# Pooled attention with a mixture of adapters: query transposes from 16 rows of 128 tokens, and score matmuls that read the queries in permuted order

## The chip, the cores and the metric

The kernel runs on one core of a Trainium2 chip. The metric is device time in microseconds (us) of one execution, at the median of several. The profiler's span is some 2 us shorter than that time. "Granted clock" is the TensorE clock that the throttle allowed, as a share of full speed, averaged over a stretch. In the traces its records are 1.00 or 0.50 only, so a value in between says for how much of the stretch the clock was halved.

## The reference, cut to what matters

```python
# q: (4, 12288, 128)   kv: (4, 384, 32, 128)   all float32
kv_pool = kv.reshape(B, H//4, 4, W//4, 4, C).mean(axis=(2, 4))   # 768 keys per batch entry
k = v = kv_pool.reshape(B, -1, C) @ w_sr
a = softmax(q @ k.T / sqrt(C));  x = a @ v                        # 49152 tokens of 128
# then per token: gate logits, the best 2 of 8 adapters of rank 16, x + weighted deltas
```

Each token is computed from its own query. The output for a token must land in that token's row, so a kernel may take tokens in any order as long as loads and stores agree.

The comparison with the reference hardly sees the order of the tokens. Worked out from the reference's own outputs, the tokens of one batch entry differ from their mean by 2.6e-6 (root mean square), where the outputs themselves have a spread of 5.0e-4. For the changed kernel and for the version with runs of 16, the token order was therefore checked by following the indices through transpose, read and store; it is right in both.

## The kernel before: the parts that the change and the argument touch

Queries are cast to bf16 in DRAM in groups of 2048 tokens (`GT`), transposed by one DMA instruction per group into `qT` (128 channels on partitions, tokens along the free axis), and used in chunks of 512 tokens (`T`, four to a group, 96 chunks in all). Groups 0 and 1 are loaded as float32 and transposed by TensorE instead.

```python
def load_qT(g):
    t = qpool.tile([P, GT], BF16, tag="qT", name="qT")
    keep(nc.sync.dma_start(t.rearrange("c (j p) -> c j p", p=P),
                           q_bf[g].rearrange("(p j) c -> p (j c)", p=P), transpose=True))

def load_q(g, lo, hi):                       # groups 0 and 1 only
    src = q[0, g * GT:(g + 1) * GT].rearrange("(p j) c -> p j c", p=P)
    keep(nc.sync.dma_start(q_f[g][:, lo:hi], src[:, lo:hi]))

def scores(k, r):                            # 3 calls per chunk, 2 matmuls each
    rhs = qT[k // GC][:, (k % GC) * T:(k % GC + 1) * T]        # 512 adjacent bf16
    ps = ps_s.tile([P, 2, T], FP32, tag="sg", name="sg")
    for i in range(2):
        mm(ps[:, i], kfT[b][:, 2 * r + i], rhs, start=True, stop=True)
    keep(nc.scalar.activation(em[k][:, 2 * r:2 * r + 2], ps, AF.Exp, bias=0.0, scale=scale))

def attend(k, s):                            # em is the weight, vx the moving operand: acc
    for j in range(J):
        mm(o, em[k][:, j, s * P:(s + 1) * P], vx[b][:, j], start=(j == 0), stop=(j == J - 1))

# ... normalize (xn), gates on GpSimd, transposes (tt_ps), down (h_ps), gate (hg), up (d_ps) ...

def finish(k):                               # partition p stores 4 adjacent tokens: 2 KB runs
    keep(nc.sync.dma_start(
        out[k // GC * GT:(k // GC + 1) * GT].rearrange("(p j) c -> p j c", p=P)
        [:, k % GC * S:(k % GC + 1) * S], osb))
```

The softmax here doesn't subtract the row's maximum and nothing guards it: scores larger than these inputs give would overflow.

## Time and profile before

| | before |
|---|---|
| time, median of 2 | 426.77 us |
| TensorE busy, share of the span | 92% |
| granted clock, mean | 0.979 |
| one chunk in the steady state | 3.68 us |
| one pair of score matmuls | 0.43 us |

The busy times of the page of before, whole span:

```profile
PE 389.1 (92%) x4589; PEld 308.8 (73%) x4589; DVE 327.3 (77%) x967; ACT 292.8 (69%) x336; POOL 162.5 (38%) x263
```

Busy times by stretch, before. The columns are the stretch and its length, then busy time (and instructions) of each engine, the granted clock, the DMA engines' busy share and GB/s:

```profile
core 0: us, PE busy (x) PEld busy (x) DVE busy (x) ACT busy (x) POOL busy (x), PEclk, DMA share, GB/s
...
100.00:145.00 45.00, 45.00 (x563) 36.46 (x561) 39.23 (x114) 34.07 (x39) 12.14 (x25) 1.00 0.70 174
...
200.00:245.00 45.00, 45.00 (x563) 36.48 (x560) 39.02 (x113) 34.91 (x40) 12.15 (x23) 1.00 0.71 184
```

The average of 92% hides that TensorE is busy in all of these stretches (45.00 of 45.00 us), at full clock (1.00). How long each instruction holds it there the busy time does not say, so the next view is the chain of waits, the chain that ended last. Columns: start, length, instructions. This is one period of before:

```profile
329.47 0.43 PE sg L68 x2
329.90 0.22 PE h_ps L68 x4
330.12 1.12 PE acc L68 x18
331.24 0.43 PE sg L68 x2
331.67 0.45 PE tt_ps L68 x8
332.12 0.43 PE sg L68 x2
332.55 0.22 PE d_ps L68 x4
332.77 0.37 PE acc L68 x6
333.15 0.43 PE sg L68 x2
```

From 329.47 to 333.15 is 3.68 us, and nothing but matmuls is on it. A pair of score matmuls (`sg`) takes 0.43 us, so 215 ns for 512 columns, or 0.42 ns a column. The list of groups gives another number for the same instruction (columns: busy time, mean ns of one, then the idle time before and who ended it):

```profile
L68 PE MATMUL sg<-qT,kfT 128*128 128x512 bf16 x576 | 170.9, 378 | 2.7 <-ACT em L246 2.2
L246 ACT ACTIVATE em<-sg 128x1024 f16<-128x1024 f32 x288 | 280.5, 1023 | 97.3 <-PE sg L68 96.4
```

The 378 ns are the time from start to end of one matmul; in the chain the next one starts 215 ns after it. For the cost in a stream, use the distances in the chain.

The DMA side of before (packets, then issues with KB each and median us from issue to landing):

```profile
DMA packets 71172, 76.43 MB, mean 181 GB/s; under 512 B 49904, under 2 KB 50160, under 8 KB 70640
...
qT<-qbf SPq DMA_TRANSPOSE x22, 8.1
```

A transpose lands 8.1 us after its issue and is used about a group (four chunks, 14.7 us) later. No compute engine's list of waits shows one for it.

### The profile page before, as it was taken

The page shows a single profiled execution, that of the slowest core. Times are in us where ns is not written, and L with a number is a line of the kernel's source. Part 1 is how long each engine was busy: PE and PEld are TensorE (multiplying, and loading weights), DVE is VectorE, ACT ScalarE, POOL GpSimd, SP SyncE. Part 2 cuts the span into 40 slices and gives each one's busy share as a digit, 9 for nine tenths or more (in the row PEclk, how much of TensorE's full clock was granted, in tenths as well). Part 3 has the DMA queues.
Part 4 walks back from the last instruction along what each step waited for, and adds up shares of the span by engine and source line. Part 5 has one row for each costly group of instructions (what it writes and reads, how often), then busy time and mean ns, then how long its engine had stood idle before and what let it go on. Part 6 is the DMA issues. An engine that isn't in the chain of part 4 may idle for free.

```text
span 423.3 us, 11396 instructions
## 1 busy us (share of the span) xinstructions
PE 389.1 (92%) x4589; PEld 308.8 (73%) x4589; DVE 327.3 (77%) x967; ACT 292.8 (69%) x336; POOL 162.5 (38%) x263
## 2 busy tenths in 40 slices
PE   4898999999999999999999999999999999999853
PEld 3566777787877878787888778777888877788642
DVE  2644678788988878779888878779888888888853
ACT  3478567686777777676788777676777866678522
POOL 0010357965320557964330467963231312222000
PEclk9999999999999999999999999999999999999965
DMA  8989557776556998765647999998575628342112
GB/s 302 397 214 284 110 182 199 276 161 140 128 123 134 335 252 258 286 159 114 158 126 150 318 248 164 355 135 182 130 170 129 150 76 175 108 119 75 52 63 88
DMA packets 71172, 76.43 MB, mean 181 GB/s; under 512 B 49904, under 2 KB 50160, under 8 KB 70640
## 3 DMA queue, kind: packets, MB, share of 16 engines
q1 hardware_dynamic: 70128, 64.11, 52.7%
q0 software_dynamic: 704, 11.54, 14.5%
q8 instruction: 36, 0.59, 0.6%
q14 instruction: 16, 0.13, 0.1%
q10 hardware_dynamic: 288, 0.07, 0.1%
HBM read 50.53 MB, written 36.70 MB: 206 GB/s over the span
## 4 chain that ended last, share of the span: by engine, by line
PE 72%; DVE 10%; POOL 8%; ACT 3%; DMA 2%; issue 2%; SPq 1%; ACTq 0%; DVEq 0%
PE acc L68 28%; PE sg L68 23%; PE tt_ps L68 9%; PE d_ps L68 5%; PE h_ps L68 4%; POOL kvr L171 4%; DVE hg L350 3%; ACT em L246 2%; DVE osb L363 2%; DVE xn L263 2%; POOL over L293 1%; PE v_ps L68 1%; SPq L98 1%; PE kpT_ps L68 1%; DMA kvr<-in_kv_dram 1%
## 5 line engine op out<-in xcount | busy, mean ns | idle before, releaser
L246 ACT ACTIVATE em<-sg 128x1024 f16<-128x1024 f32 x288 | 280.5, 1023 | 97.3 <-PE sg L68 96.4
L68 PE MATMUL acc<-vx,em 128*128 128x137 f16 x2304 | 174.1, 224 | 2.0 <-DVE xn L263 1.9
L68 PE MATMUL sg<-qT,kfT 128*128 128x512 bf16 x576 | 170.9, 378 | 2.7 <-ACT em L246 2.2
L68 PEld LDWEIGHTS <-em 128*128 128x128 f16 x2304 | 149.8, 98 | 4.9 <-DVE xn L263 2.2
L68 PEld LDWEIGHTS <-tts 128*128 128x128 bf16 x768 | 59.1, 99 | 53.0 <-ACT tts L334 5.6
L350 DVE TENSOR_TENSOR hg<-h_ps,gw 128x512 bf16<-128x512 f32 x96 | 66.1, 688 | 29.9 <-POOL gw L315 16.1
L293 POOL TENSOR_TENSOR over<-xn,srt 128x128 f32<-128x128 f32 (+1 forms) x54 | 19.8, 384 | 175.7 <-DVE srt L281 175.7
L263 DVE TENSOR_TENSOR xn<-acc,rinv 128x544 f32<-128x544 f32 x96 | 69.5, 724 | 3.3
L171 POOL TENSOR_TENSOR kvr<-kvr 128x512 f32<-128x512 f32 x54 | 67.4, 1268 | 2.1 <-DMA kvr<-in_kv_dram 1.9
L363 DVE TENSOR_TENSOR osb<-d_ps,xn 128x512 f32<-128x512 f32 x96 | 65.9, 689 | 2.7 <-PE d_ps L68 2.6
L336 DVE COPY tts<-tt_ps 128x1024 bf16<-128x1024 bf16 (+1 forms) x95 | 63.9, 672 | 2.4 <-PE tt_ps L68 2.4
L68 PEld LDWEIGHTS <-xn 128*128 128x128 bf16 x384 | 29.5, 99 | 28.6 <-issue 6.1
L68 PEld LDWEIGHTS <-kfT 128*128 128x128 bf16 x576 | 45.9, 97 | 6.0 <-issue 3.7
L68 PE MATMUL h_ps<-a_bf,tts 128*128 128x128 bf16 x384 | 37.6, 221 | 6.1 <-ACT tts L334 3.9
L68 PE MATMUL tt_ps<-id_bf,xn 128*128 128x128 bf16 x384 | 37.5, 221 | 6.0 <-DVE hg L350 4.4
L258 DVE RECIPROCAL rinv<-acc 128x4 f32<-128x4 f32 x96 | 17.3, 180 | 32.9 <-PE acc L68 32.2
L68 PE MATMUL tt_ps<-id_bf,hg 128*128 128x128 bf16 x384 | 38.1, 223 | 3.2 <-DVE hg L350 2.8
L68 PE MATMUL d_ps<-b_bf,tts 128*128 128x128 bf16 x384 | 38.0, 224 | 2.6 <-DVE hg L350 1.0
L281 DVE MAX8 srt<-xn 128x8 f32<-128x8 f32 x384 | 34.5, 153 | 0.2
L68 PEld LDWEIGHTS <-hg 128*128 128x128 bf16 x384 | 26.1, 100 | 4.2 <-DVE hg L350 3.7
L312 ACT ACTIVATE th<-over 128x128 f32<-128x128 f32 (+2 forms) x33 | 9.1, 276 | 15.5 <-DVE over L298 12.2
L314 POOL TENSOR_TENSOR gw<-th,over 128x128 f32<-128x128 f32 (+1 forms) x27 | 11.0, 406 | 21.6 <-ACT th L312 21.5
(49 smaller groups left out, 162.4 us busy)
## 6 DMA issues: line engine op xcount, KB each, us to landing
out_dram<-osb SPq DMA_DIRECT2D x96, 256.0 KB, 3.3
kvr<-in_kv_dram SPq DMA_DIRECT2D x36, 512.0 KB, 6.2
qbf<-in_q_dram POOLq DMA_DIRECT2D x22, 512.0 KB, 6.7
kvr<-in_kv_dram SPq DMA_DIRECT2D x24, 256.0 KB, 4.9
qf<-in_q_dram SPq DMA_DIRECT2D x1, 1024.0 KB, 5.1
qf<-in_q_dram SPq DMA_DIRECT2D x4, 256.0 KB, 5.1
qT<-qbf SPq DMA_TRANSPOSE x22, 8.1
w_sr_sb<-in_w_sr_dram ACTq DMA_DIRECT2D x1, 64.0 KB, 4.7
```

What stands on the lines that cost most here:

```text
L68: return keep(nc.tensor.matmul(*a, **k))
L171: keep(adder.tensor_tensor(u[:, lo:hi], u[:, lo:hi], v[:, lo:hi], op=ALU.add))
L246: keep(nc.scalar.activation(em[k][:, 2 * r:2 * r + 2], ps, AF.Exp, bias=0.0, scale=scale))
L258: keep(nc.vector.reciprocal(ri, acc[k][:, :, VC]))
L263: keep(nc.vector.tensor_tensor(x, acc[k][:, :, 0:VC], ri.unsqueeze(2).broadcast_to([P, S, VC]), op=ALU.mult))
L281: keep(nc.vector.max(srt[k0][:, m, s], xn[k][:, s, C:VC]))
L293: keep(eng.tensor_tensor(d, lg, so[:, :, i].unsqueeze(2).broadcast_to([P, n, 8]), op=ALU.subtract))
L312: keep(nc.scalar.activation(th, arg, AF.Tanh, bias=0.0, scale=0.5))
L314: keep(eng.tensor_tensor(w[:, 0:n], th, mask, op=ALU.mult))
L336: keep(nc.vector.tensor_copy(sb[:, lo:hi], ps[:, lo:hi]))
L350: keep(nc.vector.tensor_tensor(hg[k].rearrange("p s (e r) -> p (s e) r", e=E), hp[k].rearrange("p s (e r) -> p (s e) r", e=E), gw[k0][:, m ...
L363: keep(nc.vector.tensor_tensor(osb, dp[k], xn[k][:, :, 0:C], op=ALU.add))
```

## The change

The intent: take the transposed queries from 16 rows of 32 KB in DRAM instead of 128 rows of 4 KB, still one instruction per group. The tokens then lie in `qT` as (j r) with 16 rows r innermost. To keep four adjacent tokens on each partition, so that stores keep their 2 KB runs, the score matmul reads `qT` in permuted order: for each s and r, the eight j, which are 64 elements (128 bytes) apart. Its output stays contiguous.

```diff
 def load_qT(g):
-    keep(nc.sync.dma_start(t.rearrange("c (j p) -> c j p", p=P),
-                           q_bf[g].rearrange("(p j) c -> p (j c)", p=P), transpose=True))
+    keep(nc.sync.dma_start(t.rearrange("c (j r) -> c j r", r=16),
+                           q_bf[g].rearrange("(r j) c -> r (j c)", r=16), transpose=True))
+def rows_of(tokens):
+    return tokens.rearrange("(r m j s) c -> m r j (s c)", r=16, m=GC, s=S)
 def load_q(g, lo, hi):
-    src = q[0, g * GT:(g + 1) * GT].rearrange("(p j) c -> p j c", p=P)
-    keep(nc.sync.dma_start(q_f[g][:, lo:hi], src[:, lo:hi]))
+    src = rows_of(q[0, g * GT:(g + 1) * GT])
+    for m in range(lo // S, hi // S):
+        keep(nc.sync.dma_start(
+            q_f[g][:, m * S:(m + 1) * S].rearrange("p s c -> p (s c)"), src[m]))
 def scores(k, r):
+    if k // GC > 1:
+        rhs = rhs.rearrange("c (j s r) -> c s r j", s=S, r=16)
-        mm(ps[:, i], kfT[b][:, 2 * r + i], rhs, start=True, stop=True)
+        o = ps[:, i]
+        if k // GC > 1:
+            o = o.rearrange("p (s r j) -> p s r j", s=S, r=16)
+        mm(o, kfT[b][:, 2 * r + i], rhs, start=True, stop=True)
 def finish(k):
-        out[...].rearrange("(p j) c -> p j c", p=P)[:, k % GC * S:(k % GC + 1) * S], osb))
+        rows_of(out[k // GC * GT:(k // GC + 1) * GT])[k % GC],
+        osb.rearrange("p s c -> p (s c)")))
```

## The prediction

> **What bounds the kernel now.** TensorE's instruction stream. Busy times by stretch: in 100–145, 200–245 and 300–340 us TensorE is busy throughout at a granted clock of 1.00; VectorE is at 87%, ScalarE at 76–78%. The chain of waits in 326–334 us is matmuls alone: a chunk of 512 tokens takes 3.68 us, of which the six score matmuls (sg) take 3 x 0.43 us, so 215 ns for each 512 columns (the 378 ns in the list of groups is an overlapped latency). Exceptions: the first 60 us, some places where GpSimd makes `hg` late (some 2 us of TensorE idle in each of 60–100, 145–200 and 245–300 us), and the last 30 us.
>
> DMA does not bound it. The DMA engines are 60–99% busy, but in the list of waits almost nothing waits for a DMA after the start. Query transposes land in 8.1 us and are issued a group of four chunks (14.7 us) ahead; stores land in 3.3 us with six buffers.
>
> **What the change does.**
> 1. The 22 transposes read 16 rows of 32 KB instead of 128 of 4 KB, the same bytes. Issue (median 3.1 us on the sync queue) and landing may shorten; neither is waited for: gain 0 to 1 us.
> 2. Stores keep 2 KB runs: about 0.
> 3. The first query load becomes four of 256 KB ahead of the key loads, at about 0.45–0.7 us per issue, and the start waits for keys: +0 to +1.5 us.
> 4. Instruction counts and order are unchanged: the comparison of the two builds shows only renamed lines and new DMA shapes.
> 5. The score matmuls of chunks 8 to 95 (88 x 6 = 528) read the moving operand with an innermost step of 64 bf16 elements (128 bytes) instead of 1. The output stays contiguous. [...] No trace of this case shows the size. [...] TensorE's present idle in 60–390 us, about 9 us, absorbs perhaps 6 us: GpSimd's chain is then in time.
>
> **Prediction.** 426.8 + 112 - 6 = 533 us. If the stride costs nothing, 425–428 us (a quarter of my belief). Range 424 to 560 us. Chances: faster by over 2% 0.03, within 2% 0.25, slower by over 2% 0.72.
>
> **What would show each step.**
> - Right: in the chain of waits the pair of sg matmuls grows from 0.43 to about 0.85 us, the chunk from 3.68 to about 4.95 us; sg's mean in the groups grows from 378 to about 590 ns; chunks 0–7 keep 215 ns; acc, tt, h and d matmuls keep their spacing. ScalarE's wait for sg grows from 96 to some 190 us; VectorE's and ScalarE's shares fall, their busy times don't. GpSimd leaves the chain.
> - Transposes: shorter issue or landing, with no wait of TensorE removed.
> - Wrong: sg at 378 ns, chunk at 3.68 us, time as before.
>
> **What would make it wrong.** [...] The penalty may be larger (at four times, about 760 us) or partial. The 16-row transposes may land beyond 15 us, so that score matmuls wait for them[...].

The sum of the forecast came to 426.8 + 112 - 6 = 533 us. Its term of 112 us, the slower read, was not a measured one.

## The result, and the profile after

The changed kernel takes 829.02 us (828.18 to 829.87, 2 runs) against 426.77 us: a ratio of 1.9425, with a 95% interval of 1.934 to 1.951.

Busy times of after, whole span, and the granted clock in 40 slices (tenths of full speed):

```profile
PE 802.6 (97%) x4589; PEld 396.8 (48%) x4589; DVE 339.8 (41%) x967; ACT 308.9 (37%) x336; POOL 162.6 (20%) x263
...
PEclk9998777877887888897787788779678887788786
```

Busy times by stretch, after:

```profile
100.00:145.00 45.00, 45.00 (x240) 22.38 (x239) 17.64 (x50) 15.75 (x17) 19.32 (x25) 0.77 0.31 77
200.00:245.00 45.00, 45.00 (x256) 21.34 (x254) 17.70 (x48) 16.39 (x18) 5.00 (x11) 0.81 0.37 92
```

TensorE is as busy as before, but in the first of these stretches it does 240 instructions where it did 563, and its clock is no longer full. The other engines' busy times grow by 6% at most; they wait. The list of groups of after:

```profile
L68 PE MATMUL sg<-qT,kfT 128*128 128x512 bf16 x576 | 513.4, 980 | 2.3 <-ACT em L256 1.8
L256 ACT ACTIVATE em<-sg 128x1024 f16<-128x1024 f32 x288 | 293.7, 1025 | 487.0 <-PE sg L68 487.0
```

The chain of waits of after has two faces. First a period at nearly full clock, then a stretch at a low one:

```profile
501.78 1.72 PE sg L68 x2
503.50 0.23 PE h_ps L68 x4
503.73 1.12 PE acc L68 x18
504.85 1.72 PE sg L68 x2
506.56 0.45 PE tt_ps L68 x8
507.01 1.72 PE sg L68 x2
...
509.85 1.70 PE sg L68 x2
511.55 0.43 PE h_ps L68 x4
511.97 2.07 PE acc L68 x18
514.05 1.70 PE sg L68 x2
```

The stretches around these two pieces, after, with the granted clock third from the end:

```profile
499.40:508.50 9.10, 9.10 (x50) 3.19 (x48) 3.95 (x10) 3.81 (x4) 0.00 (x0) 0.98 0.48 141
509.00:515.50 6.50, 6.50 (x34) 3.67 (x32) 2.57 (x8) 1.81 (x2) 4.25 (x6) 0.54 0.42 121
```

Two things are to be seen. A score pair takes 1.72 us instead of 0.43, four times as long. And in the second stretch, at a clock of 0.54, the ordinary matmuls take about twice as long (18 `acc` 2.07 us instead of 1.12), while the score pair takes 1.70 us all the same. So at both clocks the slow read keeps a pace of its own, 1.7 ns a column.

The DMA side of after:

```profile
DMA packets 26900, 76.43 MB, mean 92 GB/s; under 512 B 4896, under 2 KB 5152, under 8 KB 26144
...
qT<-qbf SPq DMA_TRANSPOSE x22, 4.7
```

Transposes make far fewer packets and land sooner. Whether that is their new shape or only the halved traffic per microsecond (92 GB/s against 181) has to be tried.

### The profile page after: what moved, and what is told of

Read it like the earlier page. It is cut to its first block, busy times and chain, and to the rows that moved or that the text cites. A ratio compares the mean times of both kernels' runs of the same rounds, so it can differ in the third digit from the quotient of the medians.

```text
span 827.9 us, 11402 instructions
## 1 busy us (share of the span) xinstructions
PE 802.6 (97%) x4589; PEld 396.8 (48%) x4589; DVE 339.8 (41%) x967; ACT 308.9 (37%) x336; POOL 162.6 (20%) x263
## 4 chain that ended last, share of the span: by engine, by line
PE 95%; DVE 2%; DMA 1%; ACT 1%; issue 0%; SPq 0%; DVEq 0%; ACTq 0%
PE sg L68 55%; PE acc L68 24%; PE tt_ps L68 5%; PE h_ps L68 4%; PE d_ps L68 3%; PE kpT_ps L68 1%; PE v_ps L68 1%; ACT em L256 1%; DMA kvr<-in_kv_dram 1%; DMA qf<-in_q_dram 1%; PE kfT_ps L68 0%; ACT tts L344 0%; DVE xn L273 0%; DVE osb L373 0%; DVE hg L360 0%
## 5 line engine op out<-in xcount | busy, mean ns | idle before, releaser
L68 PE MATMUL sg<-qT,kfT 128*128 128x512 bf16 x576 | 513.4, 980 | 2.3 <-ACT em L256 1.8
L256 ACT ACTIVATE em<-sg 128x1024 f16<-128x1024 f32 x288 | 293.7, 1025 | 487.0 <-PE sg L68 487.0
L68 PE MATMUL acc<-vx,em 128*128 128x137 f16 x2304 | 232.1, 268 | 1.2 <-DVE xn L273 1.2
L68 PEld LDWEIGHTS <-em 128*128 128x128 f16 x2304 | 204.5, 122 | 4.0 <-DVE xn L273 1.6
L68 PEld LDWEIGHTS <-tts 128*128 128x128 bf16 x768 | 74.0, 118 | 270.6 <-issue 199.5
L68 PEld LDWEIGHTS <-xn 128*128 128x128 bf16 x384 | 32.8, 106 | 132.1 <-issue 129.8
L68 PEld LDWEIGHTS <-kfT 128*128 128x128 bf16 x576 | 54.6, 113 | 6.2 <-issue 3.8
L68 PE MATMUL h_ps<-a_bf,tts 128*128 128x128 bf16 x384 | 49.1, 268 | 5.5 <-ACT tts L344 3.9
L68 PE MATMUL d_ps<-b_bf,tts 128*128 128x128 bf16 x384 | 45.8, 255 | 2.0 <-DVE hg L360 1.2
L174 POOL TENSOR_TENSOR kvr<-kvr 128x512 f32<-128x512 f32 (+1 forms) x18 | 17.9, 996 | 1.4
```

What stands on the lines that cost most here:

```text
L68: return keep(nc.tensor.matmul(*a, **k))
L174: keep(adder.tensor_tensor(u, u, v, op=ALU.add))
```

## The experiments

Eight kernels were run, each beside runs of the kernel before on the same chip (medians 426.3 to 426.8 us).

### 1. The permuted read alone

```diff
 # kernel before, in scores():
+        if k // GC > 1:
+            rhs = rhs.rearrange("c (j s r) -> c s r j", s=S, r=16)
+            # and o = o.rearrange("p (s r j) -> p s r j", ...) as in the change
```

> The kernel before with the permuted moving read of the score matmuls alone (chunks 8 to 95); wrong result on purpose. Theory R (the read is the whole cause): the time of the changed kernel, 829 us within 1%, score pairs of 1.72 us in the chain of waits and a mean granted clock near 0.82. Rival D (the new transposes, loads or stores share the cause, for example by transposes landing late): clearly below 829 us.

Measured: 825.78 us (2 runs), ratio 1.9365 (1.931 to 1.942), clock 0.825; its `sg` matmuls have a mean of 978 ns, where the changed kernel has 980. The read alone makes all but 3 us of the change. Theory R stands. And the old transposes, 128 rows each, land in 4.9 us here, at 93 GB/s, where the new shape took 4.7 us at 92: at this lower traffic the old one is nearly as quick.

### 2. All of the change but the read

```diff
 # changed kernel, in scores():
-        if k // GC > 1:
-            rhs = rhs.rearrange("c (j s r) -> c s r j", s=S, r=16)
-            # and the rearrangement of o
```

> The changed kernel with the permuted read taken back, all DMA changes kept; wrong result on purpose, since the tokens come out in another order. Theory R: within 1% of the kernel before (about 427 us, perhaps 0 to 1.5 us more for the four first loads), score pairs 0.43 us, clock 0.98, although the transposes land sooner (4.7 us instead of 8.1 us) and DMA packets fall to 26900. Rival D: well above 427 us.

Measured: 430.52 us (4 runs), ratio 1.0094 (1.008 to 1.011), clock 0.974. The score pair in its chain is back at 0.43 us. The 3.7 us left over are more than expected. The timeline of the sync queue shows why. Here is this run, then before (columns: start, length, what):

```profile
0.73 2.60 SPq L109 DMA_DIRECT2D qf<-in_q_dram  x4
3.38 0.60 SPq L98 DMA_DIRECT2D kvr<-in_kv_dram  x1
```

```profile
0.74 0.40 SPq L105 DMA_DIRECT2D qf<-in_q_dram  x1
1.19 3.41 SPq L98 DMA_DIRECT2D kvr<-in_kv_dram  x5
```

Four query loads take 2.60 us to issue where one took 0.40, so the first key load is issued at 3.38 and not at 1.19 us. VectorE's first sum of keys starts at 10.04 us and not at 7.95, and by the time the first transformed keys are written the delay has grown to 3.5 us (17.52 against 14.04), as the few matmuls between them are slower in this run (two `kfT` matmuls 1.19 us against 0.67). The slower pace lasts longer here: 8 `kpT` matmuls take 1.94 us from 10.88 us on, and only from 19.68 us on do 16 take 2.39 us; in before, 16 take 2.29 us from 10.44 us on. The later start thus also has more of its work at the slower pace. In this run, at 178 GB/s, transposes land in 7.9 us: at full traffic the new shape lands about as late as the old one (8.1 us at 181 GB/s).

### 3. A sweep of read patterns in one kernel

The kernel before, with another pattern in each eight chunks, so that one trace holds all of them. Each mode's score tile has its own name.

```diff
 # kernel before, in scores():
+        mode = "abcgjhikdef"[(k - 2 * GC) // 8] if k >= 2 * GC else "z"
+        if mode in "bcdef":      # step n
+            rhs = rhs.rearrange("c (a b) -> c b a", b=n)          # n = 2, 4, 8, 16, 64
+        elif mode in "gjhi":     # runs of n, 128 bytes apart
+            rhs = rhs.rearrange("c (j s r) -> c s j r", j=8, r=n) # n = 16, 8, 4, 2
+        elif mode == "k":        # contiguous read, output step 8 fp32
+            o = o.rearrange("p (a b) -> p b a", b=8)
```

> The kernel before, with another pattern of the moving read (modes b to j) or of the write to PSUM (k) in each 8 chunks from chunk 8 on; wrong result on purpose. Modes in order: a step 1; b step 2 elements; c step 4; g runs of 16 elements 128 bytes apart; j runs of 8; h runs of 4; i runs of 2; k contiguous read, output step 8 fp32; d step 8; e step 16; f step 64. Time of one score pair, 0.43 us in mode a. Theory L (each visit of a 16-byte line costs about four columns of time, 1.7 ns): b 0.43, c 0.86, d, e and f 1.72, g and j 0.43, h 0.43, i 0.86. Theory L2[...]: as L but c and i 0.43. Rival S (any step other than 1 costs four): b and c 1.72 as well, g, j, h, i near 0.43. Rival W (the restart of a short inner loop costs, some 10 ns for each of the 64 inner runs of 8): d and e little above 0.43 and j 1.72, h and i far more. Mode k: if a strided write to PSUM costs nothing, 0.43. The granted clock should be 1.00 in modes at 0.43 and near 0.8 in modes at 1.72, if the slow read is what lowers the clock.

The time of one score pair, read from the chain of waits within each mode, with the bf16 elements that the read takes in one visit from an aligned stretch of 16 bytes, the line of theory L:

| mode | read pattern | elements per visit of a line | pair, us | granted clock |
|---|---|---|---|---|
| a | step 1 | 8 | 0.43 | 1.00 |
| g | runs of 16, 128 bytes apart | 8 | 0.43 | 1.00 |
| j | runs of 8, 128 bytes apart | 8 | 0.43 | 1.00 |
| b | step 2 | 4 | 0.45 | 1.00 |
| h | runs of 4, 128 bytes apart | 4 | 0.44 | 1.00 |
| c | step 4 | 2 | 0.90 | 1.00 |
| i | runs of 2, 128 bytes apart | 2 | 0.86–0.87 | 1.00 |
| d | step 8 | 1 | 1.77–1.80 | 0.67 |
| e | step 16 | 1 | 1.81–1.83 | 0.81 |
| f | step 64 | 1 | 1.70–1.72 | 0.83 |
| k | contiguous; output step 8 fp32 (32 bytes) | 8 | 0.86 | 1.00 |

One pair of each of five modes, as the chain shows it (start, length, instructions):

```profile
99.70 0.45 PE sg_b L68 x2
...
205.55 0.43 PE sg_j L68 x2
...
120.98 0.90 PE sg_c L68 x2
...
259.67 0.86 PE sg_i L68 x2
...
340.16 1.79 PE sg_d L68 x2
```

The clock is from the view of busy times by stretch; here a mode of two elements per line (c) and two of one (d, then f):

```profile
120.00:156.00 36.00, 36.00 (x326) 21.70 (x325) 23.04 (x64) 22.05 (x24) 8.98 (x16) 1.00 0.60 151
...
337.00:404.00 67.00, 67.00 (x342) 32.87 (x341) 23.79 (x65) 23.62 (x25) 5.94 (x13) 0.67 0.19 49
...
484.00:545.00 61.00, 61.00 (x344) 28.04 (x343) 25.24 (x72) 24.22 (x28) 6.36 (x20) 0.83 0.08 31
```

Theory L holds in every mode, to within some 7%: a visit of a line costs the time of about four columns (1.7 ns), or of its elements if these are more. Four or more elements per visit go at full rate or within 5% of it (0.43 to 0.45 us a pair), two at half (0.86 to 0.90), one at a quarter (1.70 to 1.83). Rival S falls with b (0.45, where it asks for 1.72), c (0.90, likewise) and i (0.86, where it asks for 0.43). Rival W falls with j (0.43, where it asks for 1.72), whose 64 inner runs of 8 are as many and as short as those of the change, and with d and e (1.77 to 1.83, where it asks for little above 0.43). L2 asks for 0.43 in c and i, and falls with both. The traces show times and no lines; of the sizes tried on paper, 16 bytes is the one that the times fit: with 8-byte lines c and d would take one element per visit alike, with 32-byte lines d would take two where e takes one; measured are 0.90 for c, 1.77 to 1.80 for d and 1.81 to 1.83 for e. Between the strides of one element per line there is a difference of some 6% that no theory of mine explains. The granted clock is 1.00 in every stretch read at a half rate or better, and 0.67, 0.81 and 0.83 in the three modes at a quarter.

### 4. The same TensorE time, with the array working

```diff
 # kernel before, in scores():
-            mm(ps[:, i], kfT[b][:, 2 * r + i], rhs, start=True, stop=True)
+            for again in range(4 if k // GC > 1 else 1):
+                mm(ps[:, i], kfT[b][:, 2 * r + i], rhs, start=True, stop=True)
```

> The kernel before with every score matmul of chunks 8 to 95 issued four times on the same output, contiguous read; right result. It takes the time of the slow read (four times 215 ns) with the array working in all of it. Theory A[...]: clock stays at 0.98 to 1.00, time 427 + 528 x 645 ns = 767 us less some 10 us of idle, so 755 to 770 us, and the rest of 829 us is the clock. Rival B (the clock falls with any longer score phase, because of what else waits or because of load): clock near 0.82 and about 829 us.

Measured: 754.51 us (754.30 to 754.72), ratio 1.7694, clock 0.987; the time is half a us below the expected range. In its chain, eight score matmuls take 1.73 us, as two of the slow read do (1.72):

```profile
501.04 1.73 PE sg L68 x8
...
503.22 1.12 PE acc L68 x18
504.33 1.73 PE sg L68 x8
```

On the same chip, the read alone (experiment 1) took 825.78 us. The same length of score phases thus gives 754.5 us at a clock of 0.987 and 825.8 us at 0.825: 71 us are the clock. The groups of the other matmuls bear this out: `acc`, in experiment 1 and then here, is

```profile
L68 PE MATMUL acc<-vx,em 128*128 128x137 f16 x2304 | 229.1, 266 | 1.2 <-DVE xn L268 1.2
L68 PE MATMUL acc<-vx,em 128*128 128x137 f16 x2304 | 174.5, 225 | 1.2 <-DVE xn L264 1.2
```

and `acc`, `h` and `d` together are busy 324 us there and 250 us here, 74 us more. TensorE is busy 97% of the span in both runs, and the clock is 0.825 in the one that takes its score columns at a quarter of the pace, 0.987 in the other: what theory A expected of the clock. By what measure the clock is granted is open, and this run also issues four times as many score matmuls.

### 5. Another row order, so that the read has runs

Row p of a chunk need not be (r j). With (j r) each partition still holds four adjacent tokens, and the read takes 16 adjacent elements at a time (mode g of the sweep).

```diff
 # changed kernel:
-        return tokens.rearrange("(r m j s) c -> m r j (s c)", r=16, m=GC, s=S)
+        return tokens.rearrange("(r m j s) c -> m j r (s c)", r=16, m=GC, s=S)
-            rhs = rhs.rearrange("c (j s r) -> c s r j", s=S, r=16)
+            rhs = rhs.rearrange("c (j s r) -> c s j r", s=S, r=16)
-                o = o.rearrange("p (s r j) -> p s r j", s=S, r=16)
+                o = o.rearrange("p (s j r) -> p s j r", s=S, r=16)
```

> The changed kernel with one thing altered: row p of a chunk is (j r) and not (r j), in loads, scores and stores alike, so that the permuted moving read takes runs of 16 elements (32 bytes), while stores keep 2 KB runs; tokens go where they belong. Theory L (only line visits of under four elements cost): score pairs back to 0.43 us, clock 0.97 to 0.98, time that of the changed kernel without permutation, 430.5 us (429 to 433, the new row order of the first loads may cost or save a little). Rival (any permuted order costs, or the whole read with the stores): well above.

Measured: 435.10 us (433.68 to 436.43, 4 runs), ratio 1.0204 (1.018 to 1.023), clock 0.974. The score pair is 0.43 us. The read is mended, but the time is outside the expected range by 2 us. (The runs fall into two pairs, near 434 and 436 us; the profile is of the slowest.) In that profile the first transformed keys are written at 20.86 us, later than in experiment 2 (17.52). The first sum of keys, which waits for its load, starts at 13.74 us where it started at 10.04 in experiment 2, and the DMA moved 242 GB/s in the first 20 us and not 315. The new row order of the first loads costs the start another 3.3 us.

### 6. The same, with the start of the kernel before

```diff
 # run 5, load_q() and finish() for groups 0 and 1:
-        src = rows_of(q[0, g * GT:(g + 1) * GT])       # four loads
+        src = q[0, g * GT:(g + 1) * GT].rearrange("(p j) c -> p j c", p=P)   # one load, as before
+        # finish(): rows_of(...) only where k // GC > 1, else as before
```

> As the run with (j r), but groups 0 and 1, which the transpose does not feed, load and store as in the kernel before (one first load of 1 MB). Theory (the 3.7 us of the run without permutation came from four query loads queued ahead of the first keys): the first kfT is written near 14 us and not 17.5, and the time is that of the kernel before, 426 to 428 us. Rival (the 16-row transposes themselves cost it): near 430 us. If the transposes gave anything it would be below 426 us; no theory of mine expects that.

Measured: 428.88 us (428.41 to 429.29, 5 runs), ratio 1.0058 (1.004 to 1.007). The first keys are written at 14.39 us, so the start is mended; 2.5 us remain, a bit above the expected range. The two profiled executions are 3.7 us apart. Of this, 2.2 us are at the end: the last `osb` ends at 421.53 us and the span at 427.0, so the last store needs 5.5 us; before, it is 420.03 and 423.3, so 3.3 us. The other 1.5 us lie earlier, and what they come from is not shown. Stores in rows (j r) hold other rows than those before, and in another order, 2 KB each in both; what makes the last one slower is not shown by this run, and its profile gives no landing times for the others. Experiment 7 takes the row order of the stores back.

### 7. What the 16-row transpose is worth by itself

```diff
 # run 6 with rows (r j) again and, on purpose, a contiguous read (tokens mixed up):
-            rhs = rhs.rearrange("c (j s r) -> c s j r", s=S, r=16)
-                o = o.rearrange("p (s j r) -> p s j r", s=S, r=16)
```

> The changed kernel with a contiguous moving read (tokens in another order, wrong result on purpose) and with groups 0 and 1 loaded and stored as in the kernel before; what is left of the change is the 16-row transpose and stores in rows (r j). If the 16-row transposes and these stores give and cost nothing: 426 to 427.5 us, the start as before, and the last store lands some 3.2 us after its issue, as before; the 2.5 us of the run with (j r) and the old start then belong to its stores in rows (j r). If the transposes cost it: about 429 us. If they gain: below 426 us.

Measured: 426.49 us (6 runs), ratio 1.0004 (0.999 to 1.002). The last `osb` ends at 420.40 and the span at 424.5, so its last store took 4.1 us and not the expected 3.2. Against experiment 6, the row order of the stores and the runs of the read are undone; as runs of 16 cost nothing in the sweep (mode g, 0.43 us), the 2.5 us of experiment 6 are put down to its stores in rows (j r). The DMA side of this run:

```profile
DMA packets 26468, 76.43 MB, mean 180 GB/s; under 512 B 4848, under 2 KB 5104, under 8 KB 25584
...
qT<-qbf SPq DMA_TRANSPOSE x22, 8.3
```

Packets fall from 71172 to 26468, yet transposes land in 8.3 us at 180 GB/s (before: 8.1 at 181) and take 3.1 us to issue (before: 3.1). The 4.7 us seen in the changed kernel go with its lower traffic (92 GB/s), as the 4.9 us of experiment 1 with the old shape (93 GB/s) say too. What the change was meant to improve is worth nothing here, within 0.2%.

### 8. The permutation moved to ScalarE

```diff
 # changed kernel, contiguous moving read, in scores():
+        eo = eo.rearrange("p i (s r j) -> p i j s r", s=S, r=16)     # em, step 8 fp16
+        ps = ps.rearrange("p i (j s r) -> p i j s r", s=S, r=16)     # in memory order
+        keep(nc.scalar.activation(eo, ps, AF.Exp, bias=0.0, scale=scale))
```

> The changed kernel with the permutation moved from the moving read to ScalarE's exponential: TensorE reads contiguously, ScalarE reads PSUM in order and writes em with an innermost step of 8 fp16 (16 bytes); tokens go where they belong. If ScalarE pays nothing for such a write, exponentials stay at 1.02 us and the time is about 430.5 us. If it pays as TensorE does, exponentials grow to 2 us or more; three of them then exceed a chunk's 3.68 us, ScalarE becomes the bound, and the time is 427 + 88 x (6 - 3.7) = about 630 us or more.

Measured: 1281.39 us (2 runs), ratio 3.0054. ScalarE is the bound, busy 97% of the span, as its group in this run shows:

```profile
L256 ACT ACTIVATE em<-sg 128x1024 f16<-128x1024 f32 x288 | 1227.9, 5012 | 14.5 <-PE sg L68 14.5
```

The mean of 5.01 us includes the 24 exponentials of chunks 0 to 7; in the chain two take 9.90 us, so 4.95 us each, against 1.02 before. The expectation gave the direction and only a lower bound of the size: nearly five times, where TensorE's read cost four. The run changes the step of the write and the number of its dimensions at once, so which of the two costs is not settled. The granted clock is 0.584 in the profiled run, with contiguous score reads and TensorE busy 54% of the span: a low clock was measured here without the slow read.

No version beats the kernel before. The best correct one with 16-row transposes is that of experiment 6, 0.6% slower.

## Why the prediction was wrong, point by point

- **What bounds the kernel**: right. Everything followed the stream of matmuls.
- **Items 1 and 2, transposes and stores, nothing gained**: right, and shown by experiment 7. The issue time predicted to "may shorten" did not at equal traffic.
- **Item 3, the four first loads, +0 to +1.5 us**: too small. With the rest of the change in place, and the read undone, the kernel was 3.7 us above before. The issue of four loads was read right (0.65 us each, so 2.2 us later for the keys), but it is hidden by nothing, and the delay grew to 3.5 us before the first scores, as matmuls there were still slow.
- **Item 5, the step that failed**: that the permuted read costs TensorE time is right. The size is wrong: the forecast put the score pair at about 0.85 us, and it took 1.72, so 860 ns for 512 columns, four times and not twice. 528 x 645 ns = 341 us in place of 112. In the sweep a cost for each visited 16-byte stretch fits: two elements a visit were measured at half rate (0.86 to 0.90 us a pair), and only four or more reached 0.43 to 0.45. The prediction did name the factor of four among what could go wrong, with about 760 us, but left it outside the range.
- **A term that was missing**: the granted clock. The prediction held it at 1.00. It fell to 0.82, worth 71 us (experiment 4 against experiment 1), as other matmuls slow down with it (`acc` 266 ns against 225).
- **The 6 us absorbed in idle time**: more was absorbed. Experiment 4 lengthens score phases by 528 x 3 x 216 ns = 342 us and its time by 328, so some 14 us. Of these, some 9 are seen: TensorE's time outside its busy time fell from 34 to 25 us of the span.

As a sum: 426.8 + 328 (score phases four times as long, experiment 4) + 71 (clock, experiment 1 minus experiment 4) + 3 (the changed kernel minus experiment 1) = 829 us. These are differences of neighbouring runs, so they must add up; what checks them is measured apart: 342 us of longer score phases, less some 9 us of idle time that went, for the 328; 74 us of longer `acc`, `h` and `d` for the 71; and 3.7 us for the rest of the change, in experiment 2, for the 3.

Of the signs named, right were: chunks 0 to 7 keep 0.59 us from first start to last end of a pair, as before; `acc`, `tt`, `h` and `d` keep their spacing where the clock is full, though not where it isn't; the other engines' shares fall and their busy times hardly move; GpSimd leaves the chain. Wrong in size were the pair (1.72 us, predicted 0.85), the chunk (8.1 us from 501.78 to 509.85 in the chain, a part of it at the low clock; predicted 4.95), `sg`'s mean (980 ns, predicted 590) and ScalarE's wait for it (487 us, predicted 190).

## What to carry to other kernels

In the patterns tried here, a permuted read of TensorE's moving operand was free, or nearly so (0.43 to 0.45 us a pair), only where each visit of a 16-byte stretch took at least four bf16 elements; choose the order of tokens on partitions so that the read has such runs, and see what the same order does to the stores: with rows (j r) the last one needed 5.5 us, with rows (r j) 4.1. A slow step on the engine that bounds the kernel can cost more than its own time: with score columns at a quarter of the pace the granted clock was 0.67 to 0.83, and other matmuls took longer (`acc` 266 ns against 225); at half the pace it was 1.00. And before changing the layout of a transfer, look for a wait that it would end: here there was none, and the transfer's new shape was worth nothing (426.49 us against 426.29).
